# A recurrence over two batch elements at once: the fourth element's row halves exchanged, its products in separate PSUM banks, and a new order of the program

## The chip, the cores and the metric

The kernel runs on one core of one Trainium2 chip. The metric is the device time of one execution in microseconds (us). The kernel before took 630.84, 633.05 and 630.84 us in three runs, a median of 630.84 us.

## What is computed

A delta-rule attention over 4 batch elements, 8 heads, 768 positions and 48 features, followed by an MLP mixer over tokens and channels. All data are 32-bit floats.

```python
k_n = k / (norm(k) + 1e-6)
for t in range(768):                       # state: 48 x 48 for each element and head
    y[t] = q[t] @ state
    state += beta[t] * outer(k_n[t], v[t] - k_n[t] @ state)
x = y.transpose(0, 2, 1, 3).reshape(4, 768, 384)
u = x + (relu(x.transpose(0, 2, 1) @ w_tok1) @ w_tok2).transpose(0, 2, 1)
out = u + relu(u @ w_ch1) @ w_ch2
```

## The kernel before

**Work.** The 768 positions of an element are cut into 12 chunks of C = 64 positions; a unit u is two chunks (128 positions) of one element with all 8 heads. For a unit, `prep` (L518) makes the scaled and turned keys and queries, `grams` (L494) multiplies keys with keys and with queries, `invert` (L707) inverts the unit lower triangles of a group of units on VectorE (for each of 30 steps, a product at L729 and a sum at L734), and `join` (L795) puts the blocks of the inverses together. What is left is sequential: in each chunk, four groups of small matmuls that hang on each other through the 48x48 states of the heads.

**The recurrence.** For the first two elements one element runs at a time: `recur` (L893), steps r0 to r23. The third and the fourth element (units 12 to 23, two units of the same positions beside each other) run together in `recur_pair` (L973), steps r24 to r35, with e = 0 for the third and e = 1 for the fourth element. One step c of the pair is this chain:

1. keys times state, `p_k` (L995): 16 matmuls of 48x64 by 48x48; VectorE subtracts the values from all of it (L1001) into `rest`, which is the tile `rw_t`.
2. queries times state into `p_y` (L1012), and the inverse times `rest` into `p_w` (L1016), 16 matmuls each, in turns; ScalarE copies `p_w` to `rw_t` (L1021).
3. keys times `rw_t` into `p_s` (L1030), and the query-key product times `rw_t` added to `p_y` (L1033), 16 each, in turns; VectorE subtracts `p_s` from the state `ss_t` (L1043; at the first step it copies, L1045).
4. ScalarE writes `p_y` out: the third element's half to the mixer's input (L1049), the fourth's to the tile `side` (L1054), from where a DMA takes it to DRAM (L1056). `fetch_last` (L1063) reads it back for the mixer.

**Quarters of TensorE.** A matmul of 64 (or 48) rows and 64 columns uses a quarter of the array: its row half follows from the partitions that its operands lie in, its column half from the partitions that it writes. `PAR` holds the two halves of the partitions, `FEATS` the 48 used rows of each, and i is the parity of the head. The operands of step 1 lie in `FEATS[i]`, and its output goes to `PAR[i ^ cc]`, with cc the parity of the chunk, for both elements: two of the four quarters. In steps 2 and 3 the two kinds of matmul that take turns have different column halves for the same rows, so that all four quarters are used. `grams` uses two quarters while it makes one chunk at a time (units below 12, jobs c and d), and four where it makes both chunks of a unit in turns (units from 12 on).

**PSUM.** Eight banks: two under the tag `prep`, two under `seq` (the recurrences), three under `mlp` (the mixer: `p_1`, `p_h`, `p_ut`, `p_c`, `p_o`, `p_o2`), and one under `warm`, which matmuls fill early in the program, with no result, to keep TensorE going. In `recur_pair` both elements' products share one bank: `p_k`, `p_y`, `p_w` and `p_s` each take one of the two `seq` banks.

**Order.** Every job is a generator, and a long text (`order`, L1555 and on) tells which job makes its next piece. Its pieces are, for example, r9 (recurrence step 9), i2 (third group of inversions), m0 and m1 (the mixers of the first two elements), T2, T3, A, F and B (the mixer of the last two elements, in another form, at the end), w (rounding of weights), k and v (loads). Each engine runs its instructions in this order and waits on semaphores where it must. The mixer's matmuls of 128x128 are what fills TensorE between the links of the recurrence: `p_1` (L1378 in `mixer`, L1199 in `token_part`), `p_h` (L1391, L1212), `p_ut` (L1401), `p_c` (L1449) and `p_o` (L1470). In the tail it is `p_r` (L1283) and `p_a`, `p_b` (L1355).

A matmul of 32-bit floats shows as two MATMUL records and two LDWEIGHTS records in the profile, so that the 16 matmuls of `p_k` are 32 records.

## Time and profile before

| what | value |
|---|---|
| three runs | 630.84, 633.05, 630.84 us |
| the profiled execution | 633.33 us |
| its span, first to last instruction | 631.5 us |
| TensorE's granted clock, mean | 0.975 |
| busy: TensorE matmul / weight loads | 603.1 us / 521.3 us |
| busy: VectorE / ScalarE / GpSimd | 453.2 / 260.4 / 109.5 us |
| read and written by DMA | 53.74 MB, 85 GB/s |

PE is TensorE's matmuls, PEld its weight loads, DVE VectorE, ACT ScalarE, POOL GpSimd, SP the engine that issues the DMAs. In a row of the timeline stand the start in us from the first instruction, the length of the group, the engine, the line, what is written and read, the shapes and the number of instructions; in brackets, how long the engine had been idle and what ended it. In a row of a window stand the length, then each engine's busy time with its number of instructions, TensorE's granted clock, the share of the DMA engines and GB/s. Consecutive matmuls overlap, so that the distance from one group's start to the next group's start is what a group costs TensorE.

The span has five stages by what runs: loads, grams and inversions of the first element (to about 50 us); the first element's recurrence beside inversions of the next (to 138); the second element's recurrence beside the first mixer (to 262); the pair's recurrence, r24 to r35, beside the second mixer (262 to 443); and the tail, which is the mixer of the last two elements (to the end).

### The profile page before, as it was taken

To read this page: it belongs to the slowest core of one execution; us is meant where nothing else is said; L and a number is where in the kernel's file an instruction comes from. 1 tells how busy PE (TensorE), PEld (TensorE's weight loads), DVE (VectorE), ACT (ScalarE), POOL (GpSimd) and SP (SyncE) were. 2 spreads that over 40 slices of the span, in tenths; PEclk is the share of its full clock that TensorE was granted. 3 is DMA by queue.
4 is the path that set the end of the run, shared out by engine and by line. 5 is a ranking of instruction groups with operands and counts; after the bars stand their busy time and mean duration, and the time that the engine had idled before them with its cause. 6 is when DMAs were issued, how large, how long until landed. Compare 5 with 4: busy or idle time off the path is not lost.

```text
span 631.5 us, 20723 instructions
## 1 busy us (share of the span) xinstructions
PE 603.1 (95%) x8724; PEld 521.3 (83%) x8724; DVE 453.2 (72%) x1091; ACT 260.4 (41%) x687; POOL 109.5 (17%) x146
## 2 busy tenths in 40 slices
PE   8489888999999999999999999999999999999998
PEld 5367776667898988977899997897796999999997
DVE  4987876977689854796577967764759666767674
ACT  7748786537522344123641204524351342321410
POOL 2337365124400211103120021010000000000000
PEclk9978897999999999999999999999999999999999
DMA  9786666656543344535435532132200000000011
GB/s 202 132 146 142 152 141 166 175 129 183 115 89 87 82 101 85 122 86 117 90 64 124 132 61 59 34 70 75 83 0 2 0 1 26 13 14 25 1 38 38
DMA packets 140012, 53.74 MB, mean 85 GB/s; under 512 B 115056, under 2 KB 134384, under 8 KB 139920
## 3 DMA queue, kind: packets, MB, share of 16 engines
q1 hardware_dynamic: 139920, 52.43, 37.6%
q8 instruction: 68, 1.11, 0.8%
q14 instruction: 24, 0.20, 0.1%
HBM read 41.19 MB, written 11.21 MB: 83 GB/s over the span
## 4 chain that ended last, share of the span: by engine, by line
PE 83%; DVE 6%; ACT 5%; DMA 2%; issue 2%; SPq 1%; POOL 0%; ACTq 0%; DVEq 0%; POOLq 0%
PE p_c L1449 16%; PE p_o L1470 13%; PE p_r L1283 13%; PE p_a L1355 7%; PE p_b L1355 6%; PE p_g L501 3%; PE p L1199 3%; PE p_h L1391 3%; PE p_h L1212 2%; PE p L1378 2%; PE p_k L995 2%; DVE sub L729 2%; DVE x L734 1%; PE p_s L1030 1%; PE p_y L1012 1%
## 5 line engine op out<-in xcount | busy, mean ns | idle before, releaser
L1449 PE MATMUL p_c<-u_t,wc 128*128 128x256 f32 x432 | 102.2, 389 | 0.0
L1449 PEld LDWEIGHTS p_c<-u_t,wc 128*128 128x128 f32 x432 | 80.7, 192 | 11.3 <-issue 0.2
L1470 PE MATMUL p_o<-wc,r 128*128 128x192 f32 x360 | 64.4, 330 | 0.0
L734 DVE TENSOR_TENSOR x<-x,sub 128x84 f32<-128x84 f32 (+24 forms) x178 | 59.1, 332 | 6.1
L729 DVE TENSOR_TENSOR sub<-x 128x84 f32<-128x84 f32 (+24 forms) x178 | 58.5, 328 | 5.8 <-DMA x<-n_dram 1.0
L1470 PEld LDWEIGHTS p_o<-wc,r 128*128 128x128 f32 x360 | 58.4, 190 | 1.2 <-issue 0.3
L1458 ACT ACTIVATE r<-p_c 128x512 f32<-128x512 f32 x36 | 21.5, 597 | 69.0 <-PE p_c L1449 62.9
L501 PE MATMUL p_g<-kq 48*64 48x128 f32 (+1 forms) x704 | 33.7, 285 | 3.3 <-ACT kq L577 3.3
L564 POOL TENSOR_TENSOR mb<-mask_c,cs 128x512 f32<-128x512 f32 x20 | 21.0, 1050 | 87.8 <-DVE cs L542 65.7
L507 DVE TENSOR_TENSOR gm<-p_g,mb 128x512 f32<-128x512 f32 x44 | 28.9, 682 | 7.2 <-PE p_g L501 6.7
L474 POOL TENSOR_TENSOR v_st<-v_st,nrm 128x384 f32<-128x384 f32 x12 | 11.1, 922 | 131.0 <-DMA v_st<-in_v_dram 114.5
L1296 DVE TENSOR_TENSOR gm<-gm,p_r 128x384 f32<-128x384 f32 x40 | 21.3, 551 | 16.7 <-PE p_r L1283 14.1
L501 PEld LDWEIGHTS p_g<-kq 48*64 48x64 f32 (+1 forms) x704 | 26.6, 139 | 7.4 <-ACT kq L577 4.3
L1296 DVE TENSOR_TENSOR kq<-kq,p_r 128x384 f32<-128x384 f32 x40 | 21.1, 551 | 15.5 <-PE p_r L1283 13.1
L286 POOL TENSOR_TENSOR wc<-w_f,d 128x384 uint32<-128x384 uint32 x24 | 24.5, 1021 | 38.3 <-issue 8.7
L1283 PE MATMUL p_r<-t_d,wc 128*128 128x192 f32 x160 | 30.8, 330 | 0.0
L1283 PEld LDWEIGHTS p_r<-t_d,wc 128*128 128x128 f32 x160 | 26.4, 190 | 1.2 <-ACT gm L1293 0.9
L1470 PE MATMUL p_o<-wc,s 128*128 128x192 f32 x144 | 26.1, 331 | 0.0
L390 DVE STREAM_TRANSPOSE kq<-pads 128x512 f32<-128x512 f32 x24 | 25.6, 1106 | 0.4 <-PE p_y L1012 0.2
L1283 PE MATMUL p_r<-pads,wc 128*128 128x192 f32 x128 | 25.4, 326 | 0.0
L1293 ACT COPY kq<-p_r 128x384 f32<-128x384 f32 x24 | 11.5, 478 | 31.5 <-PE p_r L1283 31.5
L1409 DVE TENSOR_TENSOR xb<-xb,p_o 128x192 f32<-128x192 f32 x42 | 14.6, 348 | 13.4 <-PE p_o L1470 13.1
(261 smaller groups left out, 1391.0 us busy)
## 6 DMA issues: line engine op xcount, KB each, us to landing
d<-in_moe_w_ch_dram SPq DMA_DIRECT2D x24, 384.0 KB, 3.6
v_st<-in_v_dram SPq DMA_DIRECT2D x96, 48.0 KB, 3.2
out_dram<-xb SPq DMA_DIRECT2D x23, 192.0 KB, 1.9
kst<-in_k_dram SPq DMA_DIRECT2D x64, 48.0 KB, 3.1
n_dram<-gm SPq DMA_DIRECT2D x72, 32.0 KB, 2.5
pads<-in_k_dram SPq DMA_DIRECT2D x24, 96.0 KB, 2.4
pads<-in_q_dram SPq DMA_DIRECT2D x24, 96.0 KB, 2.7
gm<-w_dram SPq DMA_DIRECT2D x72, 32.0 KB, 2.2
```

Of the source, the lines that this page charges most:

```text
L286: nc.gpsimd.tensor_tensor(out=dst.bitcast(U32), in0=f, in1=lo, op=ALU.add)
L390: nc.vector.transpose(kq_of[p // 2][:, i, :, p % 2].rearrange("f p (s g) -> f p g s", g=G), rows_of[i].rearrange("s p (g d) -> s p g d", g ...
L501: nc.tensor.matmul(p_g[PAR[i ^ cc], p], kqt[f, p, cc, 0], kqt[f, p, cc])
L507: nc.vector.tensor_tensor(out=blocks(gm_of(u))[:, :, cc, D:GW].rearrange("s p (two n) -> s p two n", two=2), in0=p_g, in1=made[u][:, :, cc ...
L729: nc.vector.tensor_tensor(out=tmp, in0=y[:, :, 0:s, s : s + 1].to_broadcast([n, k, s, w]), in1=y[:, :, s : s + 1, s + 1 : m].to_broadcast( ...
L734: nc.vector.tensor_tensor(out=y[:, :, 0:s, s + 1 : m], in0=y[:, :, 0:s, s + 1 : m], in1=tmp, op=ALU.add,)
L1283: nc.tensor.matmul(p[:, i], pieces[q // width][:, at : at + 128], f[f"u{n}"], start=first and i == 0, stop=True, skip_group_check=True,)
L1296: nc.vector.tensor_tensor(out=o, in0=o, in1=p, op=op_of(sign))
L1355: nc.tensor.matmul(p, a[:, i], w[:, i // 2, i % 2], start=first and i == 0, stop=True, skip_group_check=True,)
L1449: nc.tensor.matmul(p_c[:, k], piece_of(wc1, cb, f * 128)[:, f * 128 : (f + 1) * 128], u_t[:, cb], start=(cb == 0), stop=(cb == NCB - 1),)
L1458: nc.scalar.activation(r2[:, m], p_c, ACTF.Relu)
L1470: nc.tensor.matmul(p, a[:, m], wc2[:, m, j], start=(start and i == 0), stop=(i == NM - 1), skip_group_check=True,)
```

## The change

The fourth element's rows (e = 1, units 13, 15, ... 23) lie in the other half of the partitions: `swap(u)` is 1 for them, and the keys, values, beta and grams of this element are loaded or written with the halves exchanged. For beta this needs a tile `pick`, four small copies on GpSimd at the start, which takes the place of a strided slice of the identity. In step 1 the third element then uses two quarters of TensorE and the fourth the two others, and the matmuls go through them in turns (p, e, i instead of e, p, i). `p_k`, `p_y` and `p_s` are two tiles each, one for each element, in banks of their own: the second of `p_k` and of `p_s` under the tag `mlp`, the second of `p_y` under `warm`; the subtraction after step 1 and the one after step 3 are two instructions each, of half the width. The table of the order is another one from r8 on.

```diff
@@ -123,6 +123,14 @@
         r = slice(C * i, C * i + C)
         nc.gpsimd.tensor_copy(out=mask_c[r], in_=mask_f[r, r])
 
+    pick = const.tile([B * H, 2, B * NP], FP32, name="pick")
+    for par in range(2):
+        for n0, n1, first in ((0, (B - 1) * NP, par), ((B - 1) * NP, B * NP, 1 - par)):
+            nc.gpsimd.tensor_copy(
+                out=pick[:, par, n0:n1],
+                in_=ident[: B * H, 2 * n0 + first : 2 * n1 : 2],
+            )
+
     def tiles(name, shape, n):
         return [const.tile(shape, FP32, name=f"{name}{i}") for i in range(n)]
 
@@ -247,8 +255,7 @@
         for c in range(NQ):
             for par in range(2):
                 nc.tensor.matmul(
-                    p_b[PAR[par ^ c % 2], c], rows[:, c * C : (c + 1) * C],
-                    ident[: B * H, par : B * H : 2],
+                    p_b[PAR[par ^ c % 2], c], rows[:, c * C : (c + 1) * C], pick[:, par],
                 )
         yield
         nc.scalar.copy(beta_st.rearrange("s b p c -> s c (b p)"), p_b)
@@ -353,6 +360,9 @@
         c, e = divmod(u - JU, 2)
         return 2 + e, c
 
+    def swap(u):
+        return int(where(u)[0] == B - 1)
+
     def heads_of(src, u):
 
         b, c = where(u)
@@ -432,7 +442,7 @@
         for par in range(2):
             for cc in range(2):
                 nc.sync.dma_start(
-                    out=dst[PAR[par ^ cc], :, cc], in_=rows[par, cc]
+                    out=dst[PAR[par ^ cc ^ swap(u)], :, cc], in_=rows[par, cc]
                 )
                 yield
 
@@ -461,7 +471,7 @@
         for e, u in enumerate(us):
             rows = heads_of(v, u)
             for par in range(2):
-                nc.sync.dma_start(out=v_st[PAR[par ^ cc], e], in_=rows[par, cc])
+                nc.sync.dma_start(out=v_st[PAR[par ^ cc ^ e], e], in_=rows[par, cc])
                 yield
         assert masked.issuperset(us)
         at = place(us[0])
@@ -499,7 +509,7 @@
                 for cc, p_g in zip(chunks, p_gs):
                     f = PAR[i] if u < TU else FEATS[i]
                     nc.tensor.matmul(
-                        p_g[PAR[i ^ cc], p], kqt[f, p, cc, 0], kqt[f, p, cc]
+                        p_g[PAR[i ^ cc ^ swap(u)], p], kqt[f, p, cc, 0], kqt[f, p, cc]
                     )
             yield
         for cc, p_g in zip(chunks, p_gs):
@@ -984,34 +994,46 @@
         y2 = xbs[2][rows, cu].rearrange("s (p n) -> s p n", p=NP)
         y3 = side[rows].rearrange("s i (p n) -> s i p n", p=NP // 2)
         heads = [
-            (e, p, i, PAR[i ^ cc], PAR[1 - i])
+            (e, p, i, PAR[i ^ cc ^ e], PAR[1 - i])
             for e in range(2) for p in range(NP) for i in range(2)
         ]
         rest = rw_t
         if c > 0:
-            p_k = ps_seq([128, 2, NP, D], "p_k")
-            for n, (e, p, i, r, _) in enumerate(heads):
+            p_ks = [
+                ps_seq([128, NP, D], "p_k"), ps_mlp([128, NP, D], "p_k2"),
+            ]
+            for n, (p, e, i) in enumerate(
+                (p, e, i) for p in range(NP) for e in range(2) for i in range(2)
+            ):
                 f = FEATS[i]
-                nc.tensor.matmul(p_k[r, e, p], ops[e][1][f, p, cc, 0], ss_t[f, e, p])
-                if n % 8 == 7:
-                    keyed.add(2 * us[e] + cc)
+                nc.tensor.matmul(
+                    p_ks[e][PAR[i ^ cc ^ e], p], ops[e][1][f, p, cc, 0], ss_t[f, e, p]
+                )
+                if n == 15:
+                    keyed.update(2 * u + cc for u in us)
                 if n % 4 == 3:
                     yield
             assert ("pair", c) in scaled
-            nc.vector.tensor_tensor(out=rest, in0=p_k, in1=vsts["pair", c], op=ALU.subtract)
+            for e, p_k in enumerate(p_ks):
+                nc.vector.tensor_tensor(
+                    out=rest[:, e], in0=p_k, in1=vsts["pair", c][:, e], op=ALU.subtract
+                )
             yield
         else:
             rest = vsts["pair", c]
 
-        p_y = ps_seq([128, 2, NP, D], "p_y")
+        p_ys = [
+            ps_seq([128, NP, D], "p_y"),
+            psum.tile([128, NP, D], FP32, name="p_y2", tag="warm", bufs=1),
+        ]
         p_w = ps_seq([128, 2, NP, D], "p_w")
         for n, (e, p, i, r, o) in enumerate(heads):
             gm, kqt = ops[e]
             if c > 0:
                 f = FEATS[i]
                 nc.tensor.matmul(
-                    p_y[o, e, p], kqt[f, p, cc, 1], ss_t[f, e, p],
-                    start=(n < 2), stop=False, skip_group_check=True,
+                    p_ys[e][o, p], kqt[f, p, cc, 1], ss_t[f, e, p],
+                    start=(p == 0), stop=False,
                 )
             nc.tensor.matmul(p_w[r, e, p], gm[r, 2 * p + cc, TC], rest[r, e, p])
             if n % 8 == 7:
@@ -1023,35 +1045,36 @@
 
         on = c < NQ - 1
         if on:
-            p_s = ps_seq([128, 2, NP, D], "p_s")
+            p_ss = [ps_seq([128, NP, D], "p_s"), ps_mlp([128, NP, D], "p_s2")]
         for n, (e, p, i, r, o) in enumerate(heads):
             gm = ops[e][0]
             if on:
                 nc.tensor.matmul(
-                    p_s[PAR[i], e, p], gm[r, 2 * p + cc, 0:C], rw_t[r, e, p]
+                    p_ss[e][PAR[i], p], gm[r, 2 * p + cc, 0:C], rw_t[r, e, p]
                 )
             nc.tensor.matmul(
-                p_y[o, e, p], gm[r, 2 * p + cc, GC], rw_t[r, e, p],
-                start=(c == 0 and n < 2), stop=(n >= len(heads) - 2),
-                skip_group_check=True,
+                p_ys[e][o, p], gm[r, 2 * p + cc, GC], rw_t[r, e, p],
+                start=(c == 0 and p == 0), stop=(p == NP - 1),
             )
             if n % 8 == 7:
                 walked.add(2 * us[e] + cc)
                 yield
         if on:
-            if c > 0:
-                nc.vector.tensor_tensor(out=ss_t, in0=ss_t, in1=p_s, op=ALU.subtract)
-            else:
-                nc.vector.tensor_copy(out=ss_t, in_=p_s)
+            for e, p_s in enumerate(p_ss):
+                s = ss_t[:, e]
+                if c > 0:
+                    nc.vector.tensor_tensor(out=s, in0=s, in1=p_s, op=ALU.subtract)
+                else:
+                    nc.vector.tensor_copy(out=s, in_=p_s)
             yield
         sign = 1.0 if c else -1.0
         for i in range(2):
-            nc.scalar.mul(y2[:, :, D * i : D * i + D], p_y[PAR[1 - i], 0], sign)
+            nc.scalar.mul(y2[:, :, D * i : D * i + D], p_ys[0][PAR[1 - i]], sign)
         written.add(2 * NQ + c)
         yield
-        src = p_y.rearrange("s e (i p) n -> s e i p n", i=2)
+        src = p_ys[1].rearrange("s (i p) n -> s i p n", i=2)
         for i in range(2):
-            nc.scalar.mul(y3[:, :, :, D * i : D * i + D], src[PAR[1 - i], 1], sign)
+            nc.scalar.mul(y3[:, :, :, D * i : D * i + D], src[PAR[1 - i]], sign)
         yield
         nc.sync.dma_start(
             out=x_dram[C * c : C * c + C].rearrange("s (i n) -> s i n", i=2),
@@ -1570,52 +1593,59 @@
     w27*2 w7*2 d9*4 c9*2 f5 c9*3 t7*2 t8 r7*2 t7*2 j4*2 v4 p10*2 h5 r8*3 w29 t8*3
-    w29 w27*2 r8*2 w29*2 q3 w29 j4*2 r8 w22*4 t9*3 r8*4 t9 p10*2 w32 h5*3 j5 h5
+    w29 w27*2 r8*2 w29*2 q3 w29 j4*2 r8 w22*4 t9*3 r8*3 p9 r9 p10 r9*3 t9 v5 h5*3
...
```

On TensorE, at one step of the pair (between two pieces of `p_o` of the second mixer), stood before:

```order
L1470 MATMUL p_o_6228<-wc_115,r_5747 128x192 x3
L995 MATMUL p_k<-ss_t,kq 64x48 x16
L874 MATMUL p_x<-gm,zst 32x32 x16
L1012 MATMUL p_y<-ss_t,kq 64x48
L1016 MATMUL p_w<-rw_t,gm 64x48
L1012 MATMUL p_y<-ss_t,kq 64x48
```

Of the same step stands now, with `p_k_6279` the fourth element's tile (`p_k2`), L884 the old L874 and L1493 the old L1470:

```order
L1009 MATMUL p_k<-ss_t,kq 64x48 x2
L1009 MATMUL p_k_6279<-ss_t,kq 64x48 x2
L884 MATMUL p_x<-gm,zst 32x32 x16
L1493 MATMUL p_o_6261<-wc_120,r_5873 128x192 x3
L1034 MATMUL p_y<-ss_t,kq 64x48
L1038 MATMUL p_w<-rw_t,gm 64x48
L1034 MATMUL p_y<-ss_t,kq 64x48
```

Pairs of matmuls of the two elements now take turns, and three matmuls of `p_o` stand between `p_x` and the first `p_y`; they came later in the program before.

On VectorE, the rows of the same step before, from the state's subtraction of the step ahead of it to the first products of an inversion behind it:

```order
L1043 TENSOR_TENSOR ss_t<-ss_t,p_s 128x384
L1429 TENSOR_TENSOR s_5936<-r_5747 128x384
L1429 TENSOR_TENSOR s_5937<-s_5936,r_5747 128x384
L1429 TENSOR_TENSOR r_5747<-r_5747 128x3x128
L1409 TENSOR_TENSOR xb<-xb,p_o 128x192
L1001 TENSOR_TENSOR rw_t<-p_k,v_st 128x384
L729 TENSOR_TENSOR sub<-x 64x168
```

And now (L1066 and L1018 are the old L1043 and L1001, L739 and L744 the old L729 and L734, L1452 and L1432 the old L1429 and L1409):

```order
L1066 TENSOR_TENSOR ss_t<-ss_t,p_s 128x192
L1066 TENSOR_TENSOR ss_t<-ss_t,p_s_6219 128x192
L739 TENSOR_TENSOR sub<-x 64x184
L744 TENSOR_TENSOR x<-x,sub 64x23x8
L1452 TENSOR_TENSOR s_5972<-r_5873 128x384
L1452 TENSOR_TENSOR s_5973<-s_5972,r_5873 128x384
L1452 TENSOR_TENSOR r_5873<-r_5873 128x3x128
L1432 TENSOR_TENSOR xb<-xb,p_o 128x192
L739 TENSOR_TENSOR sub<-x 64x168
L744 TENSOR_TENSOR x<-x,sub 64x24x7
L1018 TENSOR_TENSOR rw_t<-p_k,v_st 128x192
L1018 TENSOR_TENSOR rw_t<-p_k_6279,v_st 128x192
```

Each subtraction of the recurrence is two of half the width, and two steps of the inversion have moved into this stretch.

The third place is early, on VectorE in the first element's recurrence, around the state's subtraction of step r9 (L957) and the subtraction of r10 behind it (L917), among the steps of the third inversion. Before:

```order
L734 TENSOR_TENSOR x<-x,sub 128x10x21
L957 TENSOR_TENSOR ss_t<-ss_t,p_s 128x192
L729 TENSOR_TENSOR sub<-x 128x220
L734 TENSOR_TENSOR x<-x,sub 128x11x20
L729 TENSOR_TENSOR sub<-x 128x228
L734 TENSOR_TENSOR x<-x,sub 128x12x19
L729 TENSOR_TENSOR sub<-x 128x234
L734 TENSOR_TENSOR x<-x,sub 128x13x18
L917 TENSOR_TENSOR rw_t<-p_k,v_st 128x192
```

Now, with L967 and L927 the old L957 and L917:

```order
L739 TENSOR_TENSOR sub<-x 128x220
L744 TENSOR_TENSOR x<-x,sub 128x11x20
L739 TENSOR_TENSOR sub<-x 128x228
L744 TENSOR_TENSOR x<-x,sub 128x12x19
L967 TENSOR_TENSOR ss_t<-ss_t,p_s 128x192
L739 TENSOR_TENSOR sub<-x 128x234
L744 TENSOR_TENSOR x<-x,sub 128x13x18
L739 TENSOR_TENSOR sub<-x 128x238
L744 TENSOR_TENSOR x<-x,sub 128x14x17
L927 TENSOR_TENSOR rw_t<-p_k,v_st 128x192
```

The state's subtraction of r9 stands behind two more steps of the inversion than before.

More of the change, by code (lines that the diff above doesn't have):

```diff
@@ new lines @@
+    j5 i2 r9 w4*2 r8 h5 i2*5 w4 i2 w19*2 k10 w32 p10*2 w32 v7 k12 m0*2 k11 k12 q0
+    v5*3 p10*2 r9*2 j5*2 k11*3 i2*2 r9 w4 i2 j5 i2*3 p10 v5 r9*2 d10*3 r10 v7*2 j5
+    i2*2 r10*4 w12 i2 k12 i2*2 m0 w32 k11 k12 w32 r10*2 m0 p11 k12*4 w19 p11 r10
+    c10 r10 c10 r10 w33 d10*2 q2 Y r11*4 v7 r11*3 w19 c10 q1 w30 c10 r11 k12*2
+    i2*3 r11 v6*4 i2*5 m0*3 i2*5 q5 i2 m0 p11*4 c10 p11 m0 p11*2 m0*2 k12*2 w12
+    m0*3 v6 f6*3 w12 d11 c11*2 d11*2 c11 w33 c11 d11*2 j6 p12 w12 m0 w33 w30*3
+    p12*2 f7*3 j6*2 m0 c11 j7 f6 f8 w27*2 f8 j7 f8 w15 f7 m0 w29 w33 w29 j7 r12*4
@@ new lines @@
+    w31 j8 p11 t10*3 r12 Y r12 f9 j8 f9 w21 p12 r12 f8 r13*2 w15*2 r12 w15 r13*3
+    w31*3 Y r13*2 w33 j8 w21 m0 r13 q4 p12*4 r13*2 m0*2 r14 c12 f9 j9 r14*2 w21
+    t10 w20*2 v7 r14*2 c12*2 w33 c12 r14 v8 c12*2 r14*2 w25*2 j9 r14 r15 v8 w21
+    r14 r15 w25 r15*3 w25 k13*4 w20 k13*4 p13 k13*2 w20 v8*3 m0*2 p13 w25 p13 m0
+    r15 p13 r15 p13 w27 w25 k13*2 j9 m0*4 p13 f9 w23 t12*3 p13 t12 w25 r15*3 c13*6
+    w23 k14*7 r16*5 m0 p13 m0*3 w23*4 k14 r16*2 t11 t13*2 j9*2 t11*3 w33 p14 r16*2
+    p14*2 w31 m0*3 w31 m0 w31 m0 w23 r17*2 r16 t13 r17 t13 r17*2 p14*2 m0*2 p14 i3
```

83 lines of the change are left out of this document (38 added, 45 removed).

## The prediction

> **What bounds the kernel now.** The page's busy times come first: is one engine busy nearly all the time?
>
> ```profile
> PE 603.1 (95%) x8724; PEld 521.3 (83%) x8724; DVE 453.2 (72%) x1091; ACT 260.4 (41%) x687; POOL 109.5 (17%) x146
> ```
>
> TensorE is. An average hides stages, so the windows by stage are next:
>
> ```profile
> core 0: us, PE busy (x) PEld busy (x) DVE busy (x) ACT busy (x) POOL busy (x), PEclk, DMA share, GB/s
> 50.00:108.00 58.00, 50.01 (x1505) 43.05 (x1508) 42.99 (x108) 48.67 (x134) 33.13 (x42) 0.91 0.67 157
> 108.00:138.00 30.00, 29.02 (x367) 18.73 (x363) 26.49 (x77) 11.32 (x29) 5.42 (x6) 0.93 0.64 161
> 138.00:262.00 124.00, 122.05 (x2099) 107.18 (x2098) 87.35 (x218) 52.77 (x153) 28.39 (x37) 1.00 0.48 107
> 262.00:443.00 181.00, 179.61 (x3260) 152.37 (x3258) 130.79 (x320) 60.65 (x179) 24.97 (x33) 0.99 0.39 83
> 443.00:631.00 188.00, 185.52 (x1070) 172.96 (x1068) 128.42 (x273) 54.79 (x114) 0.00 (x0) 1.00 0.06 20
> ```
>
> In the pair's stage, 262 to 443, TensorE is busy 179.61 of 181 us at a clock of 0.99. Here the chain of the recurrence waits for nothing that its filler does not cover: what shortens TensorE's work shortens the time, and what adds work to VectorE (130.79) costs nothing by itself.
>
> **The change, part by part.** *Keys times state on four quarters.* One step's `p_k` from the timeline of TensorE, with what follows; then, from the groups of a window that holds one step's `p_y` and `p_w`, these two:
>
> ```profile
> 415.64 1.14 PE L995 MATMUL p_k<-ss_t,kq 48*64 48x48 f32 x32
> 416.70 1.24 PE L1470 MATMUL p_o<-wc,s 128*128 128x192 f32 x6
> L1012 PE MATMUL p_y<-ss_t,kq 48*64 48x48 f32 x32 | 1.1, 221 | 0.0
> L1016 PE MATMUL p_w<-rw_t,gm 64*64 64x48 f32 x32 | 1.1, 221 | 0.0
> ```
>
> On two quarters 32 records take 1.14 us; on four, 64 records of the same size lie within the same 1.1 us. Less the last record's 0.22 us, that is 0.92 / 31 = 29.6 ns from record to record, and about 0.9 / 63 = 14.5 ns. `p_k` on four quarters thus takes 31 x 15.1 = 0.46 us less, and it runs in 11 of the 12 steps: **-5.0 us**. The other evidence is `grams`, which has both forms; the start of the next group tells each one's cost:
>
> ```profile
> 130.03 1.09 PE L501 MATMUL p_g<-kq 64*64 64x128 f32 x16
> 131.06 0.66 PE L572 MATMUL p_t<-ident,lent 128*128 128x128 f32 x4
> 138.75 1.10 PE L501 MATMUL p_g<-kq 64*64 64x128 f32 x32
> 139.78 0.48 PE L1449 MATMUL p_c<-u_t,wc 128*128 128x256 f32 x1
> ```
>
> 16 records on two quarters cost 1.03 us, 32 on four quarters 1.03 us: again a factor of two. In between, `p_k`'s new turns (rows 0, 1, 0, 1) have no row of their own; the bounds are 0 (still 29.6 ns) and -5.0, and I take -5.0, since both rows above are of four quarters.
>
> *The new order in the pair's stage.* Twice only `p_x` stands between `p_k` and `p_y`, and VectorE is not done in that time:
>
> ```profile
> 408.41 0.45 PE L874 MATMUL p_x<-gm,zst 32*32 32x32 f32 x32
> 408.79 0.31 PE L1012 MATMUL p_y<-ss_t,kq 48*64 48x48 f32 x2
> 409.19 0.25 PE L1016 MATMUL p_w<-rw_t,gm 64*64 64x48 f32 x1
> 408.58 0.56 DVE L1001 TENSOR_TENSOR rw_t<-p_k,v_st 128x384 f32<-128x384 f32 x1 [0.88 <-issue]
> 428.96 0.31 PE L1012 MATMUL p_y<-ss_t,kq 48*64 48x48 f32 x2
> 429.28 0.25 PE L1016 MATMUL p_w<-rw_t,gm 64*64 64x48 f32 x1
> ```
>
> `p_w` comes 0.40 and 0.32 us behind `p_y` where VectorE's 0.56 us end at 409.14. Now three `p_o` matmuls (six records, 1.0 us) stand there in addition, and the first half of the subtraction is done earlier: **-0.7 us**. The mixer's matmuls are only moved. By the printed order TensorE has 218 stretches of one tile size before and after, so that changing between tile sizes costs the same. One new tight place comes in: the last `p_s` and the next `p_k` have only 32 `p_z` matmuls between them. `p_k` there waits for two half subtractions, of which only the last is late; bounds 0 and one half (0.35 us, next rows); I take **+0.1 us**.
>
> *Halved subtractions.*
>
> ```profile
> L1001 DVE TENSOR_TENSOR rw_t<-p_k,v_st 128x384 f32<-128x384 f32 x11 | 6.1, 551 | 6.6 <-PE p_k L995 5.7 <-issue 0.9
> L1043 DVE TENSOR_TENSOR ss_t<-ss_t,p_s 128x384 f32<-128x384 f32 x10 | 5.5, 550 | 10.6 <-PE p_y L1033 8.9 <-PE p_s L1030 1.7
> L917 DVE TENSOR_TENSOR rw_t<-p_k,v_st 128x192 f32<-128x192 f32 x22 | 7.7, 350 | 6.2 <-PE p_k L910 4.8 <-POOL mb L564 1.3
> ```
>
> Two of 350 ns for one of 551: 22 times 0.15 us (11 + 10 + the copy) is 3.3 us of VectorE, which has 50 us to spare here. Cost 0; 3.3 us if the cover were gone. The Trainium skill says in "TensorEngine Tiling (Array Packing)", section "PSUM Bottleneck", that tiling speeds up the matmuls but not the reading of PSUM, which may then be the bound. By that rule the 5.0 us would come back as waits for VectorE; the stage's 130.79 of 181 us speak against it here.
>
> *Banks.* `p_k2` and `p_s2` take one of the mixer's three banks for about a microsecond each.
>
> ```profile
> L1458 ACT ACTIVATE r<-p_c 128x512 f32<-128x512 f32 x36 | 21.5, 597 | 69.0 <-PE p_c L1449 62.9 <-issue 5.9
> ```
>
> ScalarE empties a `p_c` bank in 0.6 us and waits 69 us for the next, so two banks are enough for it: cost 0; if TensorE waited for each half subtraction, 22 x 0.35 = 7.7 us, which I don't take. `p_y2`'s bank had held only the early matmuls without a result.
>
> *`pick`.* Four small copies on GpSimd:
>
> ```profile
> 1.88 0.50 POOL L124 COPY mask_c<-mask_f 64x64 f32<-64x64 f32 x2
> 5.89 0.73 POOL L286 TENSOR_TENSOR w<-w_f,d 128x256 uint32<-128x256 uint32 x1 [3.51 <-DVE w_f L282]
> 9.15 1.57 PE L249 MATMUL p_b<-ident,b_rows 32*64 32x16 f32 x48
> ```
>
> At 0.25 us each they end near 3.4, inside GpSimd's idle 3.51 us and long before `p_b`. Cost 0, or 1.0 us without that cover. The other loads only change their partitions.
>
> *The order from r8 to r13.* VectorE is the bound there, with the steps of the inversion between the links:
>
> ```profile
> 114.85 0.35 DVE L957 TENSOR_TENSOR ss_t<-ss_t,p_s 128x192 f32<-128x192 f32 x1
> 115.11 0.38 DVE L729 TENSOR_TENSOR sub<-x 128x220 f32<-128x220 f32 x1
> 116.81 0.40 DVE L729 TENSOR_TENSOR sub<-x 128x234 f32<-128x234 f32 x1
> 117.57 0.35 DVE L917 TENSOR_TENSOR rw_t<-p_k,v_st 128x192 f32<-128x192 f32 x1
> 115.34 0.67 PE L910 MATMUL p_k<-ss_t,kq 48*64 48x48 f32 x16 [0.26 <-DVE ss_t L957]
> ```
>
> The printed order puts r9's subtraction behind two more steps (116.81 - 115.11 = 1.7 us) and a rounding of weights (0.3): r10's `p_k` starts near 117 instead of 115.34. Until r11's subtraction VectorE has the same instructions in both orders, so r11 comes at the same time. Cost 0, with bounds of -1.5 (the waits of that stretch) and +2 (the 1.7 and 0.3 not made up).
>
> **The sum.** The profiled execution took 633.33 us, 2.5 above the median of 630.84. One stretch accounts for such a difference:
>
> ```profile
> 391.94 0.20 PE L1033 MATMUL p_y<-rw_t,gm 64*64 64x48 f32 x1 [1.27 <-issue]
> 392.32 2.93 PE L1449 MATMUL p_c<-u_t,wc 128*128 128x256 f32 x6
> 396.49 1.56 PE L1449 MATMUL p_c<-u_t,wc 128*128 128x256 f32 x6
> 392.50:395.10 2.60, 2.60 (x6) 1.67 (x6) 1.97 (x5) 0.00 (x0) 0.00 (x0) 0.50 0.03 6
> ```
>
> TensorE stood for 1.27 us for want of instructions, and then the granted clock was 0.50, so that six `p_c` records took 2.93 us instead of 1.56: 2.6 us together. I suppose that the median runs had about 2.5 of it less. Then 633.33 - 2.5 - 5.0 - 0.7 + 0.1 = **625.2 us**; with the whole stretch as profiled, 627.7.
>
> **Rivals.**
>
> 1. *The supply of instructions.* Queue q8 of the page moves 1.11 MB, which is about 64 bytes for each of TensorE's 17,448 records. Four quarters use them up twice as fast, and the new order has `p_y`, `p_z`, `p_s`, `p_z` and `p_k` of a step with nothing between. Against it: the stop of 1.27 us came only once in the stage. One more such stop with its slow clock is 2.6 us: 627.8.
> 2. *The freed time comes back as waits of the chain*, or `p_k` stays at 29.6 ns and the change doesn't do what it says: about 630.8. The grams speak against the second, the little filler of two links (0.40 and 0.32 us of waiting) against much of the first.
> 3. *Slower: the clock after r9.* r10's `p_k` waits behind the two moved steps, and the clock may answer as it did earlier:
>
> ```profile
> 101.00:105.00 4.00, 2.50 (x63) 2.00 (x64) 1.13 (x5) 2.11 (x7) 2.02 (x2) 0.65 0.52 127
> 105.00:109.00 4.00, 3.75 (x53) 3.12 (x54) 2.49 (x11) 2.46 (x8) 1.98 (x3) 0.50 0.64 169
> 113.00:126.00 13.00, 12.02 (x290) 9.15 (x290) 12.31 (x35) 8.08 (x22) 2.76 (x3) 1.00 0.67 161
> ```
>
> There TensorE worked 2.50 of 4 us, and the clock stayed near a half for the next 8. If 113 to 126 ran at half clock, up to 9 us of its 12.02 would be added, less what VectorE covers anyway: 625.2 + 1.3 + 9 = 635.5. It decides once TensorE stands for 1.3 us there; VectorE being the bound speaks against the full price. The Trainium skill, "TensorE: Matmul & The Clock Gate", section "HAM oscillation — how this bites in real kernels", says that the clock goes to half only after an idle gap of more than about 3.4 us. By that rule this rival would cost nothing but its wait; the 1.27 us at 391.94, with a clock of 0.50 right behind, say that less is enough.
> 4. *More gain.* The first elements' stage loses 1.5 us of its waits and the pair's stage the rest of the stop: 622.5.
>
> **How the numbers follow.** Forecast (623.5 to 627) 0.55; more gain 0.08; supply of instructions 0.14, half of it on either side of 627.7; time given back 0.11; slower 0.12. A measurement of this kernel tells about 0.5% from no change, which is 3.15 us: faster means below 627.7. Faster 0.55 + 0.08 + 0.07 = 0.70, same 0.07 + 0.11 = 0.18, slower 0.12. The range from 621.5 to 631 leaves out the slower case and the tail of the gain.
>
> **What would show it.** In the profile after, 32 records of `p_k` and `p_k2` in 0.7 us instead of 1.14, with VectorE's two 350 ns behind them; no gap between `p_y` and `p_w` at the two places; 262 to 443 shorter by 5 to 8 us with TensorE still busy to 99%; the tail's 188 us as they were. Wrong would be a `p_k` that still takes 1.1 us, waits for `p_k2`'s or `p_s2`'s bank, new stops by "issue", or a clock below 0.9 between 113 and 126.

## The result, and the profile after

The changed kernel took **628.43 us** (median of 16 executions, 624.81 to 631.20), the kernel before beside it 631.35 (16 executions, 629.72 to 636.17): a ratio of 0.9952, 95% interval 0.9931 to 0.9972. That is 2.9 us less where 5.6 had been forecast. Its profiled execution took 626.4 us (span 624.3, mean clock 0.978).

The page's busy times, and the windows by stage (length, then busy time of PE, PEld, DVE, ACT and POOL, the clock, the DMA share and GB/s; the recurrence ends earlier, so the last bounds are moved by 7 us):

```profile
PE 593.9 (95%) x8724; PEld 513.2 (82%) x8724; DVE 453.0 (73%) x1113; ACT 260.8 (42%) x687; POOL 110.2 (18%) x150
```

```profile
50.00:108.00 58.00, 49.02 (x1473) 42.32 (x1467) 42.48 (x112) 46.64 (x129) 32.89 (x41) 0.91 0.67 162
108.00:138.00 30.00, 26.85 (x369) 17.72 (x368) 25.38 (x71) 11.64 (x30) 5.94 (x8) 0.89 0.56 140
138.00:262.00 124.00, 122.96 (x2113) 108.34 (x2112) 89.85 (x221) 53.42 (x153) 29.50 (x36) 1.00 0.49 109
262.00:436.00 174.00, 172.47 (x3254) 144.89 (x3252) 129.31 (x338) 60.47 (x179) 24.05 (x33) 1.00 0.38 86
436.00:624.00 188.00, 185.41 (x1070) 172.98 (x1068) 127.71 (x272) 54.82 (x114) 0.00 (x0) 1.00 0.06 20
```

The pair's last `p_y` starts at 433.5 us where it had started at 440.4. Of these 7 us the stage itself, from its first `p_k` to its last `p_y`, gives 5.9 (table below); the rest is an earlier start. TensorE is still busy to 99% in it, the tail is as it was, and 108 to 138 has become worse: 26.85 of 30 us busy at a clock of 0.89, where it was 29.02 at 0.93.

Keys times state in the pair, from TensorE's timeline, and VectorE's two halves behind it and behind `p_s`, from the groups:

```profile
412.49 0.68 PE L1009 MATMUL p_k<-ss_t,kq 48*64 48x48 f32 x32
413.10 1.24 PE L1493 MATMUL p_o<-wc,r 128*128 128x192 f32 x6
L1066 DVE TENSOR_TENSOR ss_t<-ss_t,p_s 128x192 f32<-128x192 f32 x20 | 6.9, 352 | 7.3 <-PE p_y L1055 5.7 <-PE p_s L1052 1.0
L1018 DVE TENSOR_TENSOR rw_t<-p_k,v_st 128x192 f32<-128x192 f32 x22 | 6.7, 346 | 1.3 <-issue 0.9 <-DMA gm<-w_dram 0.4
```

32 records cost 0.61 us from start to start, where they had cost 1.06. One of the two places where `p_w` had come late (timeline, r32) now reads:

```profile
402.53 0.45 PE L884 MATMUL p_x<-gm,zst 32*32 32x32 f32 x32
402.92 1.24 PE L1493 MATMUL p_o<-wc,r 128*128 128x192 f32 x6
404.09 0.25 PE L1034 MATMUL p_y<-ss_t,kq 48*64 48x48 f32 x1
404.09 0.25 PE L1038 MATMUL p_w<-rw_t,gm 64*64 64x48 f32 x1
```

`p_w` starts with `p_y`; the gap is gone. At the other place, in r34, both start at 422.96. What TensorE waited for between 270 and 436 us is, from its waits, only this (total, times, longest). Where the profile shows nothing that it waited for, the row says `issue`; such idle time is called a stop here.

```profile
PE p_y L1055 <- issue: 1.2, 1, 1.2
PE p_s L1052 <- issue: 0.3, 1, 0.3
```

The first is the stop of 1.27 us at 391.94 before, now at 388; the second is a new place, at 417, where `p_y`/`p_w`, `p_z`, `p_s`/`p_y`, `p_z` and `p_k` follow each other without a mixer matmul. And r10's `p_k`, from the timelines of TensorE and of VectorE and two windows:

```profile
115.91 1.09 PE L920 MATMUL p_k<-ss_t,kq 48*64 48x48 f32 x16 [2.41 <-DVE ss_t L967]
114.16 0.91 DVE L739 TENSOR_TENSOR sub<-x 128x228 f32<-128x228 f32 x1
115.10 0.40 DVE L744 TENSOR_TENSOR x<-x,sub 128x228 f32<-128x228 f32 x1
115.41 0.35 DVE L967 TENSOR_TENSOR ss_t<-ss_t,p_s 128x192 f32<-128x192 f32 x1
113.00:116.00 3.00, 0.59 (x12) 0.38 (x10) 2.86 (x7) 0.97 (x3) 0.98 (x1) 0.73 0.35 58
116.00:122.00 6.00, 6.00 (x55) 3.80 (x56) 4.66 (x14) 0.74 (x2) 1.40 (x2) 0.57 0.74 168
```

VectorE makes the moved inversion steps first; TensorE stands 2.41 us, and in the 6 us behind it runs at a clock of 0.57.

### The profile page after: what moved, and what is told of

It reads as the page before. It is cut to its first block, busy times and chain, and to the rows that moved or that the text cites. A ratio compares the mean times of both kernels' runs of the same rounds, so it can differ in the third digit from the quotient of the medians.

```text
span 624.3 us, 20748 instructions
## 1 busy us (share of the span) xinstructions
PE 593.9 (95%) x8724; PEld 513.2 (82%) x8724; DVE 453.0 (73%) x1113; ACT 260.8 (42%) x687; POOL 110.2 (18%) x150
## 4 chain that ended last, share of the span: by engine, by line
PE 83%; DVE 7%; ACT 4%; DMA 3%; issue 2%; POOL 1%; SPq 0%; ACTq 0%; POOLq 0%; DVEq 0%
PE p_c L1472 16%; PE p_o L1493 14%; PE p_r L1306 13%; PE p_a L1378 7%; PE p_b L1378 6%; PE p L1222 3%; PE p_g L511 3%; PE p_h L1414 3%; PE p_h L1235 3%; DVE sub L739 2%; DVE x L744 2%; PE p L1401 2%; PE p_y L1034 2%; PE p_warm L235 1%; DMA d<-in_moe_w_ch_dram 1%
## 5 line engine op out<-in xcount | busy, mean ns | idle before, releaser
L1472 PE MATMUL p_c<-u_t,wc 128*128 128x256 f32 x432 | 100.9, 386 | 0.0
L1493 PE MATMUL p_o<-wc,r 128*128 128x192 f32 x360 | 65.8, 332 | 0.0
L744 DVE TENSOR_TENSOR x<-x,sub 128x84 f32<-128x84 f32 (+24 forms) x178 | 59.2, 333 | 6.1
L739 DVE TENSOR_TENSOR sub<-x 128x84 f32<-128x84 f32 (+24 forms) x178 | 57.5, 323 | 8.3 <-DMA x<-n_dram 3.7
L1493 PEld LDWEIGHTS p_o<-wc,r 128*128 128x128 f32 x360 | 58.3, 190 | 1.5 <-issue 0.3
L1493 PE MATMUL p_o<-wc,s 128*128 128x192 f32 x144 | 25.6, 330 | 0.0
L1432 DVE TENSOR_TENSOR xb<-xb,p_o 128x192 f32<-128x192 f32 x42 | 14.7, 349 | 14.4 <-PE p_o L1493 14.1
```

The costliest lines, as they stand in the source:

```text
L739: nc.vector.tensor_tensor(out=tmp, in0=y[:, :, 0:s, s : s + 1].to_broadcast([n, k, s, w]), in1=y[:, :, s : s + 1, s + 1 : m].to_broadcast( ...
L744: nc.vector.tensor_tensor(out=y[:, :, 0:s, s + 1 : m], in0=y[:, :, 0:s, s + 1 : m], in1=tmp, op=ALU.add,)
L1472: nc.tensor.matmul(p_c[:, k], piece_of(wc1, cb, f * 128)[:, f * 128 : (f + 1) * 128], u_t[:, cb], start=(cb == 0), stop=(cb == NCB - 1),)
L1493: nc.tensor.matmul(p, a[:, m], wc2[:, m, j], start=(start and i == 0), stop=(i == NM - 1), skip_group_check=True,)
```

## Experiments

Executions of one kernel spread over 3 to 11 us, so two kinds of reading are used. The ratios are of many executions. Beside them stands a table that is cut out of each profiled execution by the same landmarks of TensorE's timeline: A, the `p_w` of r8 that waits for ScalarE's `gm`; B, the pair's first `p_k`; C, the start of its last `p_y`. The end is that of TensorE's last matmul. Up to A all orders are the same. Kernels that are not called "two quarters", "before" or "order only" have four quarters.

| kernel | profiled us | start of A | A to B | B to C | C to end |
|---|---|---|---|---|---|
| before | 633.33 | 101.5 | 170.3 | 168.6 | 188.1 |
| changed | 626.40 | 99.5 | 171.3 | 162.7 | 187.9 |
| changed (e7) | 626.53 | 101.0 | 169.5 | 163.2 | 187.9 |
| changed (e16) | 628.18 | 99.5 | 172.0 | 163.9 | 187.9 |
| code only (e1) | 626.47 | 97.1 | 170.7 | 165.8 | 188.1 |
| order only (e2) | 632.37 | 98.8 | 172.1 | 168.4 | 187.9 |
| two quarters (e3) | 629.88 | 98.8 | 170.3 | 168.1 | 187.9 |
| two quarters (e8) | 631.34 | 98.3 | 172.7 | 167.5 | 187.9 |
| early order of before (e4) | 630.67 | 101.2 | 170.2 | 166.6 | 187.9 |
| spread (e5) | 629.82 | 101.7 | 169.7 | 165.6 | 187.9 |
| spread (e12) | 624.76 | 98.9 | 170.1 | 163.0 | 187.9 |
| spread, early order of before (e6) | 628.22 | 100.0 | 172.3 | 163.2 | 187.9 |
| two quarters, spread (e11) | 628.01 | 100.4 | 169.0 | 166.0 | 187.9 |
| tripled (e9) | 637.80 | 98.5 | 170.0 | 176.7 | 187.9 |
| tripled (e13) | 637.65 | 98.4 | 168.9 | 177.8 | 187.9 |
| tripled (e14) | 640.52 | 99.4 | 169.7 | 178.5 | 187.9 |
| two quarters, tripled (e10) | 656.23 | 100.5 | 169.3 | 193.7 | 187.9 |
| two quarters, tripled (e15) | 657.90 | 98.3 | 172.0 | 195.0 | 187.9 |

**e1, the code without the new order.** The changed kernel with the order table of before; at three places a few pieces stand later than before had them:

```diff
-    w29 w27*2 r8*2 w29*2 q3 w29 j4*2 r8 w22*4 t9*3 r8*3 p9 r9 p10 r9*3 t9 v5 h5*3
+    w29 w27*2 r8*2 w29*2 q3 w29 j4*2 r8 w22*4 t9*3 r8*4 t9 p10*2 w32 h5*3 j5 h5
...
+    p18 r24 i4 r24 p18 r25 r24 r25*2 p18 k19*6 m1*4 i4*3 m1*2 i4 r25 k19*2 v14*5
```

> The change's code with the order of before (a few loads and prep pieces of units 18, 19 and 20 stand one or two pieces later, where the code asks for it). Theory A (the four quarters give their full 5 us, and the new order loses about 2.5 us of it around r9 and r10, where p_k waits 2.41 us and the clock is halved after it): 5 us under before, about 626.3. Theory B (the four quarters are worth 5 us in p_k, but half of it comes back in the pair's stage as waits and stalls of the instruction supply; the order gives nothing): 3 us under before, about 628.4, as the whole change. The p_k records stand 14.9 ns apart in both.

Measured: 629.44 against 631.06 us, ratio 0.9985 (0.9952 to 1.0018). A's 626.3 (0.9925) lies below the interval, B's 628.4 (0.9958) inside it. Its trace has a wait for a PSUM bank that the profiles with the new order do not have (timelines of TensorE and VectorE):

```profile
337.37 0.92 PE L1472 MATMUL p_c<-u_t,wc 128*128 128x256 f32 x3 [1.67 <-DVE rw_t L1018]
336.71 0.61 DVE L1018 TENSOR_TENSOR rw_t<-p_k,v_st 128x192 f32<-128x192 f32 x2
```

`p_c`, which shares the mixer's banks with `p_k2`, waits 1.67 us until VectorE, busy with the inversion, has read `p_k2`. In the changed kernel's three profiles no wait for this subtraction over 0.2 us occurs, so that e1 is no clean measure of the quarters.

**e2, the order without the code.** Before's code with the new table:

```diff
-    w29 w27*2 r8*2 w29*2 q3 w29 j4*2 r8 w22*4 t9*3 r8*4 t9 p10*2 w32 h5*3 j5 h5
+    w29 w27*2 r8*2 w29*2 q3 w29 j4*2 r8 w22*4 t9*3 r8*3 p9 r9 p10 r9*3 t9 v5 h5*3
```

> The code of before with the new order, whole. Theory A: the wait in front of r10's p_k is there with any code, and the two waits of p_w in the pair's stage are gone: +2.5 - 0.7, about 1.8 us over before, 633.1. Theory B: within 0.7 us of before, 630.6 to 631.3.

Measured: 632.63 us, ratio 1.0032 (1.0003 to 1.0061): the new order by itself is slower, by 0.2 to 3.8 us, as theory A said.

**e3 and e8, two quarters again.** The changed kernel without the exchange; e8 is the same, later, beside the changed kernel (e7):

```diff
     def swap(u):
-        return int(where(u)[0] == B - 1)
+        return 0
...
-                    p_ks[e][PAR[i ^ cc ^ e], p], ops[e][1][f, p, cc, 0], ss_t[f, e, p]
+                    p_ks[e][PAR[i ^ cc], p], ops[e][1][f, p, cc, 0], ss_t[f, e, p]
```

and likewise in `pick`, `v_st` and `heads`.

> The changed kernel with the fourth element's rows left in the same halves as the third's: p_k of both elements on two quarters again; the banks, the halved subtractions and the new order stay. Theory A: 5.0 us over the changed kernel, 633.4, which is 2 us over before. Theory B: 2.5 us over the changed kernel, about 631. p_k's records in the trace 29.6 ns apart instead of 14.9, if it is the quarters and not the banks that halve it.

> The changed kernel with the fourth element's rows not exchanged, once more beside the changed kernel on the same chip. If the four quarters are worth their full 5.0 us: 633.4. If about 2.5 of it comes back in the pair's stage as in the first comparison: 631.

> The changed kernel once more, beside the other three on the same chip, since its executions spread over 6 us: 628.4 again, about 0.5% under before. Its profile should show the same stops near 388 and 417, of 1 to 2 us together, and p_k's records 14.9 ns apart.

Measured: 631.01 us, ratio 1.0011 (0.9984 to 1.0037), and 631.08, 0.9994 (0.9966 to 1.0022); the changed kernel again 626.99, 0.9950 (0.9924 to 0.9977). So the quarters alone are worth 1.0003 - 0.9951 = 0.0052 of 631, **3.2 us**; with the four intervals, about 1.6 to 4.9. Yet the records are as forecast. e3's `p_k` at the place of the row above:

```profile
414.29 1.14 PE L1009 MATMUL p_k<-ss_t,kq 48*64 48x48 f32 x32
```

and in each of the 11 steps the trace of the changed kernel is 0.45 to 0.46 us shorter from `p_k` to the next group than e3's and e8's: 5.0 us. It is the quarters that halve it, not the banks.

**e4, the early order of before.** The changed kernel with before's table up to the first piece of r14, and the new one, without the pieces already used, from there:

```diff
-    w29 w27*2 r8*2 w29*2 q3 w29 j4*2 r8 w22*4 t9*3 r8*3 p9 r9 p10 r9*3 t9 v5 h5*3
+    w29 w27*2 r8*2 w29*2 q3 w29 j4*2 r8 w22*4 t9*3 r8*4 t9 p10*2 w32 h5*3 j5 h5
...
```

> The changed kernel with the order of before up to the first piece of r14, and the new order's remaining pieces behind it. Theory A: the wait of 2.41 us in front of r10's p_k and the half clock after it are gone: 2 to 3 us under the changed kernel, 625.5 to 626.5. Theory B: the same as the changed kernel, 628.4 (within 1 us).

Measured: 628.08 us, 0.9966 (0.9941 to 0.9992), the changed kernel's figure: what theory A said of r10, that the early part of the new order costs 2 to 3 us, falls. The table shows why. With the new order A to B is 171.3 to 172.7 where r10's `p_k` waits long and the clock falls behind it, and 169.0 to 170.3 where not; with the old early order it is 170.3, 170.7, 170.2 and 172.3 (before, e1, e4, e6). But B to C is 3.9 us longer than in the changed kernel's first profile, though all orders are the same there. TensorE's waits from 380 to 430 us in e4, and windows:

```profile
PE p_y L1055 <- issue: 1.5, 1, 1.5
PE p_s L1052 <- issue: 0.8, 1, 0.8
```

```profile
419.00:421.00 2.00, 1.99 (x112) 1.87 (x115) 1.47 (x3) 0.64 (x3) 0.00 (x0) 0.69 0.39 78
421.00:425.00 4.00, 4.00 (x27) 3.88 (x20) 2.89 (x8) 2.71 (x10) 1.11 (x1) 0.50 0.05 16
```

The same two stops, but longer, and behind the second one the clock is halved: r34's `p_k` to r35's takes 12.33 us instead of 9.69.

**e5, e12, e6, e11: a mixer piece in each of the two places.** Two pieces of the second mixer stand ahead of `p_s` instead of behind it:

```diff
-    r30 j21 f21 r30*2 i6*2 r30*5 i6*3 m1*2 i6 r29 r31*4 v19 r31 i6*6 m1*2 r31*2
+    r30 j21 f21 r30 m1 r30 i6*2 r30*5 i6*3 m1 i6 r29 r31*4 v19 r31 i6*6 m1*2 r31*2
...
-    f22 r33*4 p22 m1 r33 j22 f23 r33*2 j22 j23 r33 v23*2 r33*3 v22 r31 s*3 j22 j23
-    v23*3 r34*4 m1*2 j23 r34 j23 r32 s*4 m1 r33*3 j23 r34*3 T2 W r34*3 T2 r34
+    f22 r33*4 p22 m1 r33 j22 f23 r33*2 j22 j23 r33 m1 v23*2 r33*3 v22 r31 s*3 j22
+    j23 v23*3 r34*4 m1 j23 r34 j23 r32 s*4 m1 r33*3 j23 r34*3 T2 W r34*3 T2 r34
```

e5 and e12 are the changed kernel with this; e6 has e4's early order besides, e11 is e3 with it.

> The changed kernel with two pieces of the second mixer (six p_c records and six p_o records) moved ahead: each now stands between the join's p_z and the p_s of a step, at the two places (near 388 and 417 us) where TensorE stops by issue, about 2.3 us behind the start of a fetch. Theory C (TensorE uses up small matmuls faster there than its instructions arrive; the stops of 1.39 and 0.43 us in the changed kernel's profile, and in some executions a halved clock behind them, are what takes back part of the four quarters' 5 us): no stop over 0.3 us at the two places, and 1.5 to 3 us less than the changed kernel, 625.5 to 627. Theory D (the stop only moves to the next dense place, or the pieces are missing as cover where they stood before): the same as the changed kernel within 0.5 us, with stops of the same sum elsewhere after 380 us.

> The changed kernel with the two moved pieces once more, beside the others on the same chip: 626.4 again, 0.8% under before, if the first result was not chance; 627.7 if it was.

> The same two moved pieces, and the order of before up to the first piece of r14. Theory C: as the one with the new early order, 1.5 to 3 us under the 628.1 that the old early order had without the moved pieces. If the early part mattered beside it (the wait of 2.41 us in front of r10's p_k), another 1 to 2 us less than with the new early order.

> The fourth element's rows not exchanged, and the two pieces of the mixer moved into the two places of the stops. Theory C: the stops take back part of the four quarters' gain, so that without them two quarters against four stand the full 5 us apart: 631 or a little less, against 626.2 for four quarters with the same moved pieces. Theory D (the stops cost both alike): 629.5, about 3.3 apart as before.

Measured: e5 626.38 us, 0.9920 (0.9890 to 0.9950); e12 626.04, 0.9920 (0.9891 to 0.9949); e6 626.42, 0.9935 (0.9911 to 0.9959); e11 630.77, 0.9986 (0.9958 to 1.0013). Beside the changed kernel's 0.9952 and 0.9950 the two moved pieces are worth 0.3%, 2 us, twice alike (about 0.2 to 3.6 by the four intervals): **e5's kernel has the lowest ratio of all**, and beats before by 0.5 to 1.1%. The early order makes no difference here either. Four quarters against two are now 0.0066 of 631, 4.2 us, apart (about 2.0 to 6.4), nearer to 5 than the 3.2 above, but not told apart from it. Of the two stops, e12's waits from 380 to 430 us leave one, at another place, so theory D has a part in it:

```profile
PE p_o L1493 <- issue: 1.0, 1, 1.0
```

e5 and e6 have one there too, of 0.75 and 0.38 us. e11, on two quarters, has no stop over 0.2 us in the whole stage; that is one profile.

**e9, e10, and the further profiles e13, e14, e15: the quarters tripled.** Every `p_k` matmul three times over, into the same place, so that the result stays; e10 and e15 are the same on two quarters.

```diff
-            for n, (p, e, i) in enumerate(
-                (p, e, i) for p in range(NP) for e in range(2) for i in range(2)
+            for n, (p, m, e, i) in enumerate(
+                (p, m, e, i)
+                for p in range(NP) for m in range(3) for e in range(2) for i in range(2)
```

> The changed kernel with p_k's matmuls made three times over (the same products into the same places, 96 records instead of 32 in each of the 11 steps), so that what four quarters are worth is tripled. Theory E (the quarters give their full 0.45 to 0.46 us in a step and nothing of it comes back): 64 more records of 14.9 ns in 11 steps, 10.5 us over the changed kernel, about 638; the difference from the same on two quarters 3 x 5.0 = 15 us. Theory C (a third or so comes back because instructions arrive more slowly than four quarters use them up): the 96 records have stops by issue in them or behind them, records more than 15 ns apart on the average, and the difference from the two quarters is about 10 us.

> The same three times over with the fourth element's rows not exchanged, p_k on two quarters: 64 more records of 29.6 ns in 11 steps, 20.8 us over the 631 of the two quarters, about 652. With theory E 15 us over the one with four quarters, with theory C about 10.

Measured: 643.63 us, 1.0184 (1.0147 to 1.0221), and 653.94, 1.0363 (1.0324 to 1.0403): 10.3 us apart by the medians, 11.3 by the ratios (about 7.9 to 14.7). By the timings that is theory C's figure, with E's 15 just outside. A tripled `p_k` of each:

```profile
418.49 1.61 PE L1010 MATMUL p_k<-ss_t,kq 48*64 48x48 f32 x96
```

```profile
417.29 3.00 PE L1010 MATMUL p_k<-ss_t,kq 48*64 48x48 f32 x96
```

Less the last record's 0.22 us, 95 spacings of 14.6 and 29.3 ns. The quarters keep their rate where no stop falls into the group. e9's profiled execution was the quickest of its six, 637.8 us at a mean clock of 0.983; the other five took 642.71 to 645.24 at 0.965 to 0.976.

> The tripled p_k on four quarters, one more profile: five of its six timed executions took 642.7 to 645.2 us, while the profiled one took 637.8. If instructions and the clock are what takes back 5 us: an execution near 643 shows, beside the 14.7 ns of p_k's records, 5 us more of stops by issue and of halved clock in the pair's stage than the execution of 637.8 (which had 3.8 us of stops by issue there). If it is something else: the same stops as there, and the 5 us elsewhere (the start's transfers, waits for VectorE).

> The same kernel, a further profile with the same expectations, since an execution may fall on 638 again.

> The tripled p_k on two quarters, one more profile. If the slower use of instructions spares it the stops: under 2 us of stops by issue and of halved clock in the pair's stage in an execution near 650 to 654. If it has as much of them as the four quarters, the supply does not tell the two apart.

Measured: 637.65, 640.52 and 657.90 us. None of the profiles is of an execution near 643, so that question stays open. Four quarters now stop inside `p_k` (e13's timeline), and the clock falls behind the last of their stops (window):

```profile
314.42 0.77 PE L1010 MATMUL p_k<-ss_t,kq 48*64 48x48 f32 x40
316.45 1.03 PE L1010 MATMUL p_k<-ss_t,kq 48*64 48x48 f32 x56 [1.26 <-issue]
427.00:431.00 4.00, 4.00 (x97) 3.95 (x90) 0.48 (x2) 3.15 (x12) 0.24 (x1) 0.65 0.02 4
```

The stops by issue from 262 us on are 4.7 us together in e13 (1.26, 1.51, 1.93) and 3.9 in e14; in e15 they are 3.5 (0.69, again inside `p_k`, 1.40, 1.40), with the clock at 0.91 in 400 to 450, and in e10 2.2. So two quarters are not spared them. In these five profiles B to C is 177.7 us on the average with four quarters and 194.3 with two, 16.6 apart: the profiles, unlike the timings, do not show that any of the 15 is given back. But the two on two quarters spent 10.2 us of the stage at the half clock and the three others 3.4, so that 16.6 is no clean figure either.

**e16, the changed kernel once more.**

> The changed kernel, one more profile: its two profiled executions took 626.4 and 626.5 us, under the medians of 628.4 and 627.0. An execution near 628.5 should show 2 us more of stops by issue or of halved clock than the 1.8 and 2.0 us of stops in those two, if that is what parts the median from the forecast.

Measured: 628.18 us, close to the median. Against e7, the quicker of the other profiles from A on, A comes 1.5 us earlier, A to B is 2.5 us longer (r10's `p_k` waits 2.08 us, and the halved clock follows), and B to C 0.7. The stops by issue are no larger (0.8 and 0.3), so they are not what parts this execution from the quicker ones. In the pair's stage TensorE has a wait for VectorE instead (timelines of VectorE and TensorE):

```profile
333.71 0.19 DVE L739 TENSOR_TENSOR sub<-x 128x30 f32<-128x30 f32 x1 [1.22 <-DMA x<-n_dram]
335.54 0.93 DVE L744 TENSOR_TENSOR x<-x,sub 128x108 f32<-128x108 f32 x1
336.39 0.34 DVE L1432 TENSOR_TENSOR xb<-xb,p_o 128x192 f32<-128x192 f32 x1
336.79 1.24 PE L1493 MATMUL p_o<-wc,r 128*128 128x192 f32 x6 [0.79 <-DVE xb L1432]
```

VectorE came to the next inversion before its blocks were back from DRAM, waited 1.22 us, and the mixer's add that frees `p_o`'s bank stands behind the inversion's steps. VectorE waits for these blocks on two quarters as well, 0.2 to 0.7 us, so this place does not show that the quarters are the reason. A load of keys does. In e5 ScalarE waits for it as the first row says; in e3, on two quarters, the same instruction has no wait (ScalarE's timelines). In e5 the norms and turns behind it come late, TensorE waits for them (its waits from 270 to 440 us), and then the clock is lower (windows):

```profile
319.35 0.52 ACT L539 ACTIVATE ksq<-kst 128x384 f32<-128x384 f32 x1 [2.84 <-DMA kst<-in_k_dram]
315.57 0.52 ACT L539 ACTIVATE ksq<-kst 128x384 f32<-128x384 f32 x1
```

```profile
PE p_g L511 <- DVE kq L400: 1.0, 1, 1.0
```

```profile
323.00:325.00 2.00, 1.32 (x25) 1.35 (x29) 1.94 (x4) 0.19 (x1) 0.98 (x2) 0.71 0.24 36
325.00:330.00 5.00, 5.00 (x95) 4.43 (x88) 2.35 (x5) 1.51 (x4) 0.00 (x0) 0.78 0.30 48
```

All 18 profiles together show it: ScalarE waits for this load in 10 of the 11 with four quarters, 0.25 to 2.84 us, and in none of the seven with two by more than 0.1 us. The load is no slower. Where the trace has its landing, its last piece takes 2.4 to 3.1 us from issue to landing with four quarters and 2.3 to 3.1 with two, but ScalarE is ready for it 1.0 to 2.5 us after that issue instead of 2.3 to 3.5. The faster chain arrives earlier at a transfer that became no faster. TensorE itself waits over 0.2 us for what hangs on it in two of the eleven only (e5, and e6 with 0.8 us).

## Why the prediction was wrong

**`p_k` on four quarters, -5.0: the step that failed.** The records were forecast rightly, 31 spacings of 14.9 ns for 29.6 and 0.45 us in each of 11 steps. The step from there to the time, that all of it lies on the path and nothing gives it back, is what the timings contradict: the term measured 3.2 us by the ratios (1.6 to 4.9), 4.2 with the moved pieces (2.0 to 6.4), and 11.3 of 15 when tripled (7.9 to 14.7). The first and the third leave the forecast out, the second does not.

The miss of 3.2 us (628.4 for 625.2) is then, by the medians and ratios, 1.8 from this term, 0.8 from the new code and order without the quarters (e3 and e8: +0.2 where -0.6 was forecast), and 0.5 from the kernel before, whose median over 16 executions is 631.35 and not 630.84.

Where the 1.8 us go was not settled. In the profiles of like order (changed against e3 and e8) B to C is 4.5 us shorter on the average, nearly all of the 5; over all eight untripled profiles of four quarters and five of two it is 164.2 against 167.7, 3.5 us. The stops by issue do not tell the two apart: those over 0.2 us in the pair's stage add up to 1.1 to 1.4 us in the changed kernel's three profiles, and to 1.3 and 1.1 in e3's and e8's. What the quarters do bring is the late load of keys (10 of 11 profiles against none of 7); it cost TensorE about 1 us in two of them. Single profiles show more that can take time back: a stop with a halved clock (e4), a wait for VectorE (e16), the bank (e1, in the old order). What each takes on the average is not shown.

**The new order, -0.7 + 0.1: failed as well.** The two waits of 0.40 and 0.32 us went, as forecast. But with before's code the new order costs 0.32% (0.03 to 0.61), and with the new code on two quarters it comes out at nothing (1.0011 and 0.9994). What it costs was not taken apart. Two candidates are the new dense place at 417, which stops for 0.25 to 0.83 us in most profiles with the new order there, and the wait before r10 (below), which e2's profile has with its halved clock.

**The stop at 390, -2.5: right in size, wrong in reason.** It was taken for an accident of the profiled execution. It is in every profile of untripled kernels without the moved pieces, 0.8 to 1.5 us; only the halved clock behind it, 1.4 us of the 2.6, is rare. The profiled 633.33 us is 2.0 above the median of 631.35, and its start alone was 2.0 us late: its A came at 101.5 us, and the mean over all 18 profiles is 99.5. That the correction came out near is luck.

**Halved subtractions, `pick`, 0: nothing speaks against it.** VectorE has 1.3 us of waits in front of L1018 where it had 6.6 at L1001, so its slack has shrunk, but no wait of TensorE for these halves stands in the changed kernel's pair stage. The halves and the banks are also what parts e3 and e8 from e2, and those two are 0.3% quicker, which is within the noise. **Banks, 0**: right in the new order, 1.67 us at one place in the old (e1). That is of the kind that the section "PSUM Bottleneck" of the Trainium skill's "TensorEngine Tiling (Array Packing)" warns of: the copy out of PSUM, not the matmul, may become the bound. In e1 the two readings take only 0.61 us; they are late because the inversion's steps stand ahead of them on VectorE.

**The order from r8 to r13, 0 (-1.5 to +2): right.** e4 against the changed kernel and e6 against e5 show no gain from the old order. The mechanism of rival 3 is real, though: in 5 of 14 profiles of the new order a wait of 1.5 to 2.4 us is followed by a halved clock, and A to B is 171.3 to 172.7 us instead of 168.9 to 170.3 in the other nine. In one of the nine (e14) the wait was 2.24 us and the clock stayed full, so the wait alone does not do it. With the halved clock it is 2 us, not the 10 that the rival was priced at, and the nine are no slower than the old order's four.

**Rivals.** Rival 1, with 627.8 us, came nearest in size, but not by its reason: stops were seen, and moving filler into them gained 2 us, yet two quarters have as many, and an extra stop with a slow clock behind it stands in one untripled profile alone (e4). Rival 2, the freed time that comes back as waits of the chain, is borne out in part by the late load of keys. The forecast had taken neither into its likeliest case.

## What to carry to other kernels

A matmul group that is halved saves its time only as long as the transfers and the other engines keep up with the chain: price what the faster engine will reach too early, not only the records. Where several groups of small matmuls meet, a large one between them is worth trying; here two such moves gained about 2 us. And before a profiled execution is corrected to the median, compare its start with that of other executions: here 2 us of difference lay in the first 100 us, where nothing looked odd.

## What the runs showed of the hardware

- Two stops of 1.5 and 0.8 us within 30 us (e4), or one wait of 2.4 us (the changed kernel), were followed by 4 to 6 us at a clock of 0.50 to 0.57; one stop of 1.27 us (before) by 2.6 us at 0.50. A stop of 1.2 us in the changed kernel and a wait of 2.24 us in e14 were followed by none. So the length of a single stop does not decide it. The Trainium skill, "TensorE: Matmul & The Clock Gate", section "HAM oscillation — how this bites in real kernels", gives as the rule that idle gaps should not be over about 3.4 us; none of the gaps named here was as long, and shorter ones were enough, so the measurement decides.
- All 34 stops by issue of over 0.2 us from 262 us to the pair's end, in the 18 profiles, end 2.2 to 2.9 us behind the start of a transfer of 16 KB on queue q8, which carries instructions. That points to the supply of instructions; they occur with two quarters as with four.
- Over the executions on record the mean clock lies between 0.965 and 0.986, and within each kernel the lower ones tend to go with the longer times: the changed kernel's two quickest of the 16, 624.81 and 625.86 us, are its only ones at 0.984 and 0.981.
- Matmuls of 48x64 by 48x48 in 32-bit floats keep 14.6 ns a record on four quarters over 96 records, and 29.3 ns on two.
